# Attention with mixture of experts on one core: router constants at launch, a held load, padded router weights, seven warm-ups, a later split order and a single last eviction

## The chip, the cores and the metric

The kernel runs on one core of one Trainium2 chip. The metric is device time in microseconds of one launch, from runs of the same program; lower is better. The engines are TensorE (PE, with its weight loads as PEld), VectorE (DVE), ScalarE (ACT), GpSimd (POOL) and SyncE (SP), whose queue issues nearly all loads.

## The reference

Causal attention over 4 batches of 12 heads, 448 positions and 64 features, and then a mixture of 8 experts over the 1792 tokens that it leaves, 768 to 1024 to 768 features. A token goes to one expert only: all logits are sorted, and each in turn assigns its token to its expert if the token is still free and the expert has fewer than 224 tokens.

```python
scores = np.where(mask, -1e9, scale * q @ k.T)
attn = exp(scores - max); attn = attn / (sum + 1e-9)
x = (attn @ v) as [1792, 768]
order = np.argsort(-(x @ w_gate).flatten())
for idx in order:
    tok, e = idx // 8, idx % 8
    if assigned[tok] >= 0 or counts[e] >= 224:
        continue
    assigned[tok] = e; counts[e] += 1
for e in range(8):
    m = assigned == e
    out[m] = np.maximum(x[m] @ w1[e], 0.0) @ w2[e]
```

## The kernel before, in words

**Order of work.** One class, `Schedule`, is a list planner. Each piece of work is a task with an engine, a duration, a priority, a latency that its users see and the tasks that it waits for. `run` simulates the engines with these numbers and calls the tasks in the order that comes out, so each engine gets a fixed instruction stream, carried out in order. The durations and latencies are written by hand. A load's last number but one in `weights` (0.95 or 2.5) is the latency that the planner assumes between a weight load's slot on the DMA engines and the first use. A changed number changes the order in which instructions stand on the engines, never what they compute.

**Attention** works on 24 pairs of heads (pair 0 to pair 23). Queries and keys of a pair are one load of 512 KB into `raw` (two pairs to a tile, four tiles); pair 0's comes in three pieces (L217, L207), the first of 576 columns, 288 KB. SP's queue issues them in the order pair 0's pieces, pair 1, pair 2, V of pair 0 (`v`, L224), pair 3, V of pair 1, and then loads of two pairs each. For each pair TensorE makes scores (L236, L244), VectorE adds the mask and takes the row minimum of the negated scores (L253), ScalarE takes exponentials with their sums (L260), GpSimd shifts a block of them (L275) and collects the sums (`rs`, L269 and L270), VectorE takes reciprocals (L325), TensorE transposes the probabilities (L290), VectorE or ScalarE copies them to `PT` (L294, L296), and TensorE multiplies them by V (L318). Ahead of the first scores TensorE runs `WARM` matmuls of 512 columns on zeros (L183). The router's logits of finished pairs are matmuls against `WG` (L390), a padded array [128, 6, 32] of router weights: GpSimd clears it and two DMAs on its own queue fill it (L196 to L198).

**Router constants.** `route_constants` is a generator. Its first step is a group of GpSimd iotas, memsets and selects (L684 to L699: `w`, `kf`, `trif`, `iof`, `tvf`, `on`); its later steps are small VectorE instructions on them: `tri`, `io`, `tv` (L702 to L706), `top` (L709 to L713), `kk` (L720). `extras` gives these steps to the planner as tasks of low priority on VectorE, one after the other, and the GpSimd group comes out of the first of them:

```python
more = route_constants(self.nc, self.gc, self.k, self.cs)
n = 4 + len({d.key for ds_ in DIGITS for d in ds_})
out = [(lambda: next(more, None), False)] * n
```

**Experts.** For each expert in turn the router decides in rounds of digits which expert's threshold to set (matmuls L886 to L903, decision `cd`, `most`, `cw`, `tx`, `cut`, `gq`, `run`, L895 to L951), then its tokens are gathered (L1258), turned (L1284), split into a high and a low half (`xhl`), multiplied by the first matrix, passed through relu (L1329, `HH`, and L1341, `HL`), multiplied by the second matrix (`second`, L1353) and scattered (L1376). An expert's weights are 8 chunks of 768 KB (`wr`): 0 to 3 are the first matrix, 4 to 7 the second. Each chunk is split: ScalarE's CAST makes the high half `wh` (L1243), then three VectorE subtractions make the low half `wl` (L1249). Expert 0's first matrix is used unsplit (L1314); its chunks 4 to 7 are split like all others. While expert 0 is multiplied, the router already decides on expert 1. The results of the second matrix leave PSUM through ScalarE (L1361), but for the last expert's second half, where each 384 columns go as 192 by ScalarE and 192 by VectorE (L1359), and a scatter follows for each.

## Time and profile before

| | us |
|---|---|
| median of 3 runs | 459.64 (458.16 to 461.03) |
| the profiled execution | 460.4 |
| its span, first to last instruction | 458.7 |
| TensorE busy | 445.2 (97%) |
| VectorE busy | 357.8 (78%) |
| ScalarE busy | 285.2 (62%) |
| GpSimd busy | 78.6 (17%) |

The profiled execution is one of its own, with 1.7 us outside its span. Attention lasts to about 140 us, the first routing to about 160 us, the experts to the end. In a row of the timeline the first number is the start within the span, the second the time of the group, then engine, line, operation, tiles (written <- read), shape, and the count; brackets give how long the engine had been idle and what released it. Rows that stand together may overlap, since a group's time includes the pipeline's.

### The profile page before, as it was taken

What the parts mean: (1) busy time and instruction counts of PE and PEld (TensorE: products, weight loads), DVE (VectorE), ACT (ScalarE), POOL (GpSimd) and SP (SyncE); (2) the same over time, 40 slices, a digit from 0 to 9 for tenths busy, and PEclk for the clock granted to TensorE, in tenths of its full rate; (3) what the DMA queues carried; (4) which work ended last, traced back from release to release, by engine and by line L of the source; (5) the groups of instructions that cost most, each with busy time, mean ns of one, the idle gap of its engine ahead of it and who ended that gap; (6) DMA issues with size and microseconds to landing.
All of it is one profiled execution on the core that took longest, in us unless ns stands there. A gap on an engine that the chain in (4) does not pass through costs nothing.

```text
span 458.7 us, 11572 instructions
## 1 busy us (share of the span) xinstructions
PE 445.2 (97%) x4367; PEld 382.9 (83%) x4367; DVE 357.8 (78%) x1213; ACT 285.2 (62%) x710; POOL 78.6 (17%) x196
## 2 busy tenths in 40 slices
PE   8989999999999999999999999999999999999994
PEld 4767776767677598899998999899999999999994
DVE  4798888879888557899998999999995793874500
ACT  5989999999979023546635644744662855655310
POOL 5222131312130201003003003011026101001001
PEclk9999999999999999999999999999999999999998
DMA  7974585480004874977488578848749768661001
GB/s 246 419 300 172 189 304 218 160 312 3 2 1 141 237 271 120 345 231 246 138 275 259 156 256 237 301 158 240 275 131 317 248 219 266 234 206 51 12 16 44
DMA packets 19479, 91.20 MB, mean 199 GB/s; under 512 B 2272, under 2 KB 4832, under 8 KB 18144
## 3 DMA queue, kind: packets, MB, share of 16 engines
q1 hardware_dynamic: 16272, 79.21, 51.3%
q0 software_dynamic: 2672, 11.04, 7.6%
q8 instruction: 34, 0.56, 0.5%
q10 hardware_dynamic: 480, 0.23, 0.2%
q14 instruction: 21, 0.17, 0.1%
HBM read 79.45 MB, written 11.01 MB: 197 GB/s over the span
## 4 chain that ended last, share of the span: by engine, by line
PE 29%; issue 21%; DVE 12%; DMA 2%; POOL 2%; ACT 1%; POOLq 0%; ACTq 0%
PE po L1353 13%; PE ph L1319 6%; DVE wl L1249 5%; PE ph L1323 3%; DMA wr<-in_w 2%; DVE G L784 2%; POOL out L1376 2%; PE ph L1314 2%; PE rt L886 1%; PE po L1314 1%; PE ph L1284 1%; DVE hs L1337 1%; DVE xio L379 1%; DVE xhl L1302 1%; PE ph L1276 1%
## 5 line engine op out<-in xcount | busy, mean ns | idle before, releaser
L1249 DVE TENSOR_TENSOR wl<-wr,wh 128x512 fp32r<-128x512 f32 x180 | 115.9, 681 | 11.4 <-ACT wh L1243 11.4
L1243 ACT CAST wh<-wr 128x1536 fp32r<-128x1536 f32 x60 | 88.9, 1483 | 54.7 <-DMA wr<-in_w 36.1
L1319 PE MATMUL ph<-xhl,wh 128*128 128x448 f32 x336 | 109.5, 379 | 0.0
L260 ACT ACTIVATE P<-Sm,mx 128x320 f32<-128x320 f32 (+3 forms) x168 | 87.6, 534 | 9.0 <-DVE mx L253 7.1
L1323 PE MATMUL ph<-xhl,wl 128*128 128x224 f32 x336 | 89.0, 265 | 0.0
L1353 PE MATMUL po<-wh,HH 128*112 128x384 f32 x256 | 68.3, 343 | 0.0
L1353 PE MATMUL po<-wh,HL 128*112 128x384 f32 x256 | 67.8, 341 | 0.0
L1319 PEld LDWEIGHTS ph<-xhl,wh 128*128 128x128 f32 x336 | 63.1, 188 | 5.2 <-issue 0.7
L1353 PE MATMUL po<-wl,HH 128*112 128x384 f32 x256 | 67.2, 338 | 0.0
L1323 PEld LDWEIGHTS ph<-xhl,wl 128*128 128x128 f32 x336 | 64.2, 191 | 0.0
L318 PE MATMUL s<-PT,v 128*64 128x64 f32 (+3 forms) x672 | 46.7, 290 | 1.5 <-DVE PT L296 1.5
L236 PE MATMUL s<-raw 64*128 64x320 f32 (+2 forms) x288 | 47.1, 442 | 0.1
L318 PEld LDWEIGHTS s<-PT,v 128*64 128x64 f32 x672 | 32.3, 138 | 14.6 <-issue 8.6
L1353 PEld LDWEIGHTS po<-wl,HH 128*112 128x112 f32 x256 | 44.1, 175 | 0.3
L1353 PEld LDWEIGHTS po<-wh,HL 128*112 128x112 f32 x256 | 43.3, 175 | 0.2
L1353 PEld LDWEIGHTS po<-wh,HH 128*112 128x112 f32 x256 | 43.0, 175 | 0.3
L1258 POOL DMA_INDIRECT xio<-xd,idx x16 | 20.7, 1295 | 125.7 <-DVE acc L984 114.0
L253 DVE CUSTOM_DVE_ANT_0 Sm<-s,MK 128x320 f32<-128x320 f32 (+2 forms) x72 | 33.2, 486 | 9.3 <-PE s L236 8.9
L1337 DVE TENSOR_TENSOR hs<-ph,hc 128x224 f32<-128x224 f32 x56 | 21.6, 386 | 22.5 <-ACT hc L1333 22.2
L1376 POOL DMA_INDIRECT out<-xio,idx x15 | 15.5, 1036 | 128.1 <-ACT xio L1361 126.6
L1329 ACT ACTIVATE HH<-hs 128x224 fp32r<-128x224 f32 x56 | 21.9, 391 | 23.7 <-DVE hs L1337 23.7
L236 PEld LDWEIGHTS s<-raw 64*128 64x128 f32 x288 | 28.7, 187 | 6.7 <-DVE PT L296 2.2
(186 smaller groups left out, 669.9 us busy)
## 6 DMA issues: line engine op xcount, KB each, us to landing
wr<-in_w SPq DMA_DIRECT2D x64, 768.0 KB, 5.0
raw<-in_qk SPq DMA_DIRECT2D x10, 1024.0 KB, 10.7
v<-in_v SPq DMA_DIRECT2D x11, 896.0 KB, 9.8
xd<-xio SPq DMA_DIRECT2D x2, 1152.0 KB
xd<-xio SPq DMA_DIRECT2D x3, 576.0 KB, 3.5
raw<-in_qk SPq DMA_DIRECT2D x3, 512.0 KB, 7.8
v<-in_v SPq DMA_DIRECT2D x2, 448.0 KB, 8.8
xd<-xio SPq DMA_DIRECT2D x2, 192.0 KB, 5.2
```

The costliest lines, as they stand in the source:

```text
L236: self.nc.tensor.matmul(ts[sd][:, o:o + m], q[:, QS[i]:QS[i] + P], k, start=True, stop=True)
L253: self.nc.vector.tensor_tensor_reduce(Sm[:, QO[i] + sd * m:QO[i] + sd * m + m], self.S.pop((pp, sd, i)), mk, -0.125, 3.0e38, OP.add, OP.mi ...
L260: self.nc.scalar.activation(X[:, s], Sm[:, s], AF.Exp, bias=mx[:, o], scale=-1.0, accum_out=rw[:, o])
L318: self.nc.tensor.matmul(self.AV[pp][sd * 64:sd * 64 + 64, w:w + m], v[:, j if j < 3 else 3 + (3, 2, 0, 1)[j - 3], :], PT[:, o:o + m], star ...
L1243: self.nc.scalar.copy(hi, self.R[p, c])
L1249: self.nc.vector.tensor_sub(lo[:, s], self.R[p, c][:, s], hi[:, s].bitcast(F32))
L1319: nc.tensor.matmul(t[:, :2 * CAP], hi[:, s], x[:, d].rearrange("p z t -> p (z t)"), start=d == 0, stop=False)
L1323: nc.tensor.matmul(t[:, :CAP], lo[:, s], x[:, d, 0], start=False, stop=d == 5)
L1329: self.nc.scalar.activation(self.HH[p][:, f], self.P[p, f][:, :CAP], AF.Relu)
L1337: self.nc.vector.tensor_tensor(t, self.P[p, f][:, :CAP], self.Hc.pop((p, f)), op=OP.add)
L1353: self.nc.tensor.matmul(self.T[p, "o", u][z][:, :384], a[p][:, f, u * C:u * C + C], w[:, o:o + 384], start=f == 0 and n == 0, stop=f == 7 ...
L1376: s = self.nc.gpsimd.indirect_dma_start(out=out, in_=rows, in_offset=None, out_offset=bass.IndirectOffsetOnAxis(ap=ap, axis=0))
```

## The change

Six edits. (1) `WARM` goes from 10 to 7. (2) Pair 2's load waits until pair 0's first half load has landed; SP's queue holds everything behind it meanwhile. (3) The padded router weights are made on the host, as [128, 6, 32], and one load of 96 KB on SP's queue, behind V of pair 1, replaces the clearing and the two DMAs on GpSimd; the logits' matmuls wait for it. (4) The GpSimd group of the router constants is issued in `Attention.__init__`, ahead of the router's own memsets, and the extras are one step shorter. (5) The planner's latency of expert 0's chunks 4 to 7 is 2.5 in place of 0.95. (6) The last expert's second half leaves PSUM in one ScalarE copy per 384 columns.

```diff
--- before.py
+++ after.py
@@ -33,7 +33,7 @@
 W = 1024
 LATE = 12
 PIECES = {14: 3, 17: 3, 20: 3, 22: 2, 23: 1}
-WARM = 10
+WARM = 7
 FILL = 0.217
 SETS = ((0, 4), (4, 4), (8, 4), (12, 4), (16, 4), (20, 2), (22, 2))
 BIG = 1.0e30
@@ -193,9 +193,9 @@
         for z in range(2):
             self.nc.gpsimd.tensor_copy(self.MQ[64 * z:64 * z + 64], self.MK[64 * z:64 * z + 64, S - 128 + 64 * z:S - 64 + 64 * z])
         self.WG = self.cs.tile([128, 6, 32], F32, name="WG")
-        nc.gpsimd.memset(self.WG, 0.0)
-        nc.gpsimd.dma_start(self.WG[0:64, :, 0:E], wgP[0])
-        nc.gpsimd.dma_start(self.WG[64:128, :, E:2 * E], wgP[1])
+        self.wgP = wgP
+        self.more = route_constants(nc, gc, k, self.cs)
+        next(self.more)
 
     def bank(self):
         return self.ps.tile([P, 512], F32, name="s", bufs=8)
@@ -205,17 +205,25 @@
             self.raw = self.ld.tile([128, 2, W], F32, name="raw")
         o = p0 % 2
         if p0:
-            self.nc.sync.dma_start(self.raw[:, o:o + w], self.qk[:, p0:p0 + w])
+            a = self.nc.sync.dma_start(self.raw[:, o:o + w], self.qk[:, p0:p0 + w])
+            if p0 == 2:
+                self.tc.add_manual_dep(a.ins, self.gate.ins.name, mybir.DependencyInfo(mybir.DependencyClass.Sync, mybir.DependencyReason.DATA),
+                                       reason="first loads land first")
         else:
             self.nc.sync.dma_start(self.raw[:, 0, QS[2]:], self.qk[:, 0, QS[2]:])
         for u in range(w):
             self.QK[p0 + u] = self.raw[:, o + u]
 
+    def load_wg(self):
+        self.nc.sync.dma_start(self.WG, self.wgP)
+
     def load0(self):
         self.raw = self.ld.tile([128, 2, W], F32, name="raw")
         self.QK[0] = self.raw[:, 0]
         for a, b in ((P, QS[2]), (0, P)):
-            self.nc.sync.dma_start(self.raw[:, 0, a:b], self.qk[:, 0, a:b])
+            d = self.nc.sync.dma_start(self.raw[:, 0, a:b], self.qk[:, 0, a:b])
+            if a:
+                self.gate = d
 
     def load_v(self, g, u0=0, n=4):
         if u0 == 0:
@@ -485,6 +493,7 @@
                 prev = got[p] = add("DMA", 0.9 if p else 0.4, lambda p=p: self.load(p, 1), [prev], 9.0, 2.2)
             else:
                 prev = gotv[p] = add("DMA", 0.9, lambda p=p: self.load_v(0, 2 * p, 2), [prev], 9.0, 2.2)
+        prev = self.wg = add("DMA", 0.25, self.load_wg, [prev], 9.0, 2.2)
         for g in range(1, NP // 2):
             free = []
             if g >= 4:
@@ -627,7 +636,7 @@
         for p0, m in SETS:
             if p0 + m - 1 == pp:
                 pr = 5.9 - 0.1 * pp
-                t = self.pe(0.95, lambda: self.logits_mm(p0, m), [self.xts[p0 + u] for u in range(m)] + self.room(1), 3)
+                t = self.pe(0.95, lambda: self.logits_mm(p0, m), [self.xts[p0 + u] for u in range(m)] + [self.wg] + self.room(1), 3)
                 c = self.add("ACT/DVE", {"ACT": 0.42, "DVE": 0.56}, lambda e: self.logits_cp(e, p0, m), [t], pr + 0.3)
                 self.ring.append([c])
                 self.lts = c
@@ -659,8 +668,8 @@
                 return
 
     def extras(self, rt):
-        more = route_constants(self.nc, self.gc, self.k, self.cs)
-        n = 4 + len({d.key for ds_ in DIGITS for d in ds_})
+        more = self.more
+        n = 3 + len({d.key for ds_ in DIGITS for d in ds_})
         out = [(lambda: next(more, None), False)] * n
         self.G = self.cs.tile([P, REST, 128], BF, name="Ge")
         e = rt.early(self.G, self.wk)
@@ -1106,7 +1115,7 @@
                 deps += self.use[g - 4] if g < 8 else self.lo[g - 4]
             if p == 0 and c > 0:
                 deps.append(self.again)
-            self.got[g] = add("DMA", 2.185, lambda p=p, c=c: self.fetch(p, c), deps, 4.0 - 0.01 * g, 0.95 if p == 0 else 2.5, 1.1)
+            self.got[g] = add("DMA", 2.185, lambda p=p, c=c: self.fetch(p, c), deps, 4.0 - 0.01 * g, 0.95 if g < 4 else 2.5, 1.1)
             if g < 4:
                 self.lo[g] = [self.got[g]] * 3
                 continue
@@ -1205,12 +1214,7 @@
                            6.0 - 0.5 * p)
                 self.use.setdefault(g, []).append(prev)
             if f == 7:
-                if p == E - 1 and u == 1:
-                    a = [add(e, 0.3, lambda p=p, u=u, z=z, h=h, c=c: self.evict(p, u, z, h, c), [prev], 9.0)
-                         for z in zs for h, (e, c) in enumerate((("ACT", self.nc.scalar.copy),
-                                                                 ("DVE", self.nc.vector.tensor_copy)))]
-                else:
-                    a = [add("ACT", 0.41, lambda p=p, u=u, z=z: self.evict(p, u, z), [prev], 9.0) for z in zs]
+                a = [add("ACT", 0.41, lambda p=p, u=u, z=z: self.evict(p, u, z), [prev], 9.0) for z in zs]
                 puts.append(a)
                 if len(zs) == 1:
                     a = a + [half]
@@ -1353,11 +1357,7 @@
             self.nc.tensor.matmul(self.T[p, "o", u][z][:, :384], a[p][:, f, u * C:u * C + C], w[:, o:o + 384],
                                   start=f == 0 and n == 0, stop=f == 7 and n == 2)
 
-    def evict(self, p, u, z, h=None, copy=None):
-        if h is not None:
-            s = slice(h * 192, h * 192 + 192)
-            copy(self.IO[p][:, 2 + u, z * 384:z * 384 + 384][:, s], self.T[p, "o", u][z][:, s])
-            return
+    def evict(self, p, u, z):
         self.nc.scalar.copy(self.IO[p][:, 2 + u, z * 384:z * 384 + 384], self.T[p, "o", u][z][:, :384])
 
     def halves(self, p):
@@ -1413,10 +1413,13 @@
     v = np.pad(v, ((0, 0), (0, 0), (0, 64), (0, 0))).reshape(B, H, NC, 2, 64, D)
     own = np.stack([v, np.concatenate([v[:, :, :, :1], np.zeros_like(v[:, :, :, 1:])], axis=3)], axis=2)
     v = np.stack([own[:, 0::2], own[:, 1::2, :, :, ::-1]], axis=2).reshape(B, H, 2 * NC, 128, D)[:, :, [0, 1, 2, 4, 5, 6, 7]]
+    wg = np.zeros((2, D, 6, 4, E), np.float32)
+    for z in range(2):
+        wg[z, :, :, z] = inputs["moe_w_gate"].reshape(6, 2, D, E)[:, z].transpose(1, 0, 2)
     arrays = {
         "in_qk": np.ascontiguousarray(qk.transpose(1, 0, 2)),
         "in_v": np.ascontiguousarray(v.transpose(3, 0, 1, 2, 4)),
-        "in_wg": np.ascontiguousarray(inputs["moe_w_gate"].reshape(6, 2, D, E).transpose(1, 2, 0, 3)),
+        "in_wg": np.ascontiguousarray(wg.reshape(128, 6, 32)),
         "in_w1": np.ascontiguousarray(inputs["moe_w1"].reshape(E, 6, 128, 4, 256).transpose(0, 2, 3, 1, 4)).reshape(
             E, 128, 4, 1536),
         "in_w2": np.ascontiguousarray(inputs["moe_w2"].reshape(E, 4, 2, 128, DM).transpose(0, 3, 1, 2, 4)).reshape(
```

TensorE's and ScalarE's order in the attention is the same but for the three warm-ups. On VectorE the constants' steps stand one place earlier. The first piece is VectorE between pair 2's last row minimum `mx` and the copies `PT` (`rs` is pair 2's sums; `tri`, `io`, `tv`, `top` are the constants). Before:

```order
L253 ISA mx 128x1
L325 RECIPROCAL rs<-rs 128x8
L702 CAST tri<-trif 128x128
L704 TENSOR_SCALAR io<-iof 128x224
L706 CAST tv<-tvf 128x14
L296 COPY PT<-s 128x6x64
L296 COPY PT<-s 128x7x64
```

After, in the same place:

```order
L261 ISA mx 128x1
L711 CAST tri<-trif 128x128
L713 TENSOR_SCALAR io<-iof 128x224
L715 CAST tv<-tvf 128x14
L333 RECIPROCAL rs<-rs 128x8
L718 TENSOR_SCALAR top<-kf 128x128
L720 TENSOR_SCALAR kkx<-top 128x128
L721 TENSOR_TENSOR top<-top,kkx 128x128
L722 MEMSET top 128x1
L304 COPY PT<-s 128x6x64
L304 COPY PT<-s 128x7x64
```

The three casts of constants moved ahead of the reciprocal, and `top`'s four instructions ahead of the two copies.

The second piece is VectorE at expert 1's decision, beside expert 0's matrices (`wl` is the low half of expert 0's chunk 4, `HL` the low half of its relu). Before:

```order
L895 TENSOR_SCALAR cd_119<-rt 64x8
L1249 TENSOR_TENSOR wl<-wr,wh 128x512
L909 TENSOR_REDUCE most<-rt 128x1
L911 SCALAR_TENSOR_TENSOR cw<-rt,most,w_418 128x8
L913 TENSOR_REDUCE tx<-cw 128x1
L915 TENSOR_SCALAR cut<-kw,most 128x14
L921 TENSOR_SCALAR ei<-tx 128x1
L917 TENSOR_SCALAR cut<-kw,most 128x14
L940 SCALAR_TENSOR_TENSOR gq<-tm,tx,cut 128x28
L944 SCALAR_TENSOR_TENSOR run<-on,gq 128x28
L1341 SCALAR_TENSOR_TENSOR HL<-ph,HH 128x224
L951 TENSOR_REDUCE pos<-rt 128x14
```

After:

```order
L904 TENSOR_SCALAR cd_133<-rt 64x8
L918 TENSOR_REDUCE most<-rt 128x1
L920 SCALAR_TENSOR_TENSOR cw<-rt,most,w_108 128x8
L922 TENSOR_REDUCE tx<-cw 128x1
L924 TENSOR_SCALAR cut<-kw,most 128x14
L930 TENSOR_SCALAR ei<-tx 128x1
L926 TENSOR_SCALAR cut<-kw,most 128x14
L949 SCALAR_TENSOR_TENSOR gq<-tm,tx,cut 128x28
L953 SCALAR_TENSOR_TENSOR run<-on,gq 128x28
L1345 SCALAR_TENSOR_TENSOR HL<-ph,HH 128x224
L1253 TENSOR_TENSOR wl<-wr,wh 128x512
L960 TENSOR_REDUCE pos<-rt 128x14
```

The split of chunk 4 moved from ahead of the whole decision to behind `run` and one `HL`. On ScalarE the CAST of chunk 5 stands behind three relus of expert 0 in place of two, and that of chunk 7 behind the casts of `xhl`. From expert 1 on, the order is shuffled in many places, with the same number of instructions.

## Rows read from the trace of the kernel before

**Rows 1.** Busy time by stretch: us, PE, PEld, DVE, ACT, POOL, granted clock, DMA share, GB/s.
```profile
5.00:10.00 5.00, 4.89 (x34) 2.42 (x32) 3.36 (x19) 2.83 (x11) 2.49 (x6) 1.00 1.01 344
10.00:20.00 10.00, 9.58 (x134) 6.81 (x132) 8.96 (x43) 10.00 (x36) 1.58 (x7) 1.00 1.01 408
60.00:80.00 20.00, 20.00 (x326) 14.76 (x321) 16.64 (x65) 19.28 (x65) 5.13 (x19) 1.00 0.67 247
250.00:300.00 50.00, 49.46 (x422) 45.36 (x421) 49.04 (x159) 29.25 (x47) 4.48 (x6) 1.00 0.74 232
```

**Rows 2.** Waits of TensorE: who waited for whom, us in total, times, longest.
```profile
PE s L318 <- DVE PT L296: 1.5, 1, 1.5
...
PE rt L947 <- DVE gq L940: 1.0, 1, 1.0
```

**Rows 3.** Timeline of the launch, 1 to 11 us.
```profile
1.30 4.45 PE L183 MATMUL s<-zero 128*128 128x512 bf16 x10 [1.30 <-DVE zero L180]
...
5.04 0.69 POOL L198 DMA_DIRECT2D WG<-in_wg  x1
5.68 1.89 PE L236 MATMUL s<-raw 64*128 64x320 f32 x12
...
7.17 0.56 ACT L260 ACTIVATE P<-Sm,mx 128x320 f32<-128x320 f32 x1 [4.86 <-DVE mx L253]
...
7.93 1.17 PEld L236 LDWEIGHTS s<-raw 64*128 64x128 f32 x12 [0.24 <-DMA raw<-in_qk]
7.94 1.89 PE L236 MATMUL s<-raw 64*128 64x320 f32 x12
...
10.95 0.29 POOL L275 COPY P<-P 64x128 f32<-64x128 f32 x1 [3.46 <-ACT P L260]
```

**Rows 4.** DMA issues, loads of raw: queue, count, KB each, median us to landing.
```profile
raw<-in_qk SPq DMA_DIRECT2D x3, 512.0 KB, 7.8
...
raw<-in_qk SPq DMA_DIRECT2D x1, 288.0 KB, 3.0
```

**Rows 5.** Timeline of pair 2 to pair 4, 21 to 31 us.
```profile
21.50 0.15 POOL L684 IOTA w<- 128x8 f32 x1
...
22.69 1.52 POOL L693 IOTA iof<- 128x256 f32 x1
22.76 1.53 DVE L702 CAST tri<-trif 128x128 f16<-128x128 f32 x1 [1.10 <-POOL trif L690]
...
24.73 0.20 POOL L699 MEMSET on<- 128x128 f16 x1
24.80 0.18 DVE L706 CAST tv<-tvf 128x14 f16<-128x14 f32 x1 [0.29 <-POOL tvf L697]
24.89 1.08 DVE L296 COPY PT<-s 128x384 f32<-128x384 f32 x2
...
26.03 1.12 PE L318 MATMUL s<-PT,v 128*64 128x256 f32 x20 [1.48 <-DVE PT L296]
...
26.47 0.56 ACT L260 ACTIVATE P<-Sm,mx 128x320 f32<-128x320 f32 x1 [1.05 <-POOL rs L270]
...
30.08 0.29 DVE L712 TENSOR_TENSOR top<-top,kkx 128x128 int32<-128x128 int32 x1
```

**Rows 6.** Timeline of expert 1's decision, 173 to 177 us.
```profile
173.48 1.47 ACT L1243 CAST wh<-wr 128x1536 fp32r<-128x1536 f32 x1 [2.48 <-DMA wr<-in_w]
...
173.71 0.17 PE L898 MATMUL rt<-cd,on 128*128 128x8 f16 x1
...
174.99 0.69 DVE L1249 TENSOR_TENSOR wl<-wr,wh 128x512 fp32r<-128x512 f32 x1 [1.41 <-ACT wh L1243]
...
176.88 0.17 PE L947 MATMUL rt<-gq,tri 128*128 128x28 f16 x1 [1.01 <-DVE gq L940]
```

**Rows 7.** Timeline of the tail, 444 to 455 us.
```profile
444.03 0.86 ACT L1361 COPY xio<-po 112x384 f32<-112x384 f32 x2 [7.01 <-PE po L1353]
...
452.56 0.36 DVE L1359 COPY xio<-po 112x192 f32<-112x192 f32 x1 [3.81 <-PE po L1353]
452.95 0.32 ACT L1359 COPY xio<-po 112x192 f32<-112x192 f32 x1 [3.85 <-DVE xio L1359]
...
453.55 0.94 POOL L1376 DMA_INDIRECT out<-xio,idh  x1 [3.14 <-ACT xio L1359]
```

## The prediction

> **What bounds the kernel now.** I read the busy time by stretch first. Between 60 and 80 us TensorE is busy 20.00 of 20.00 us, and between 250 and 300 us 49.46 of 50.00, with VectorE at 49.04 beside it [rows 1]. A busy TensorE is a pipelined figure of the profile, so it doesn't say that every matmul runs at its best; it does say that TensorE waits for almost nothing there. So what counts is where TensorE stands when such a stretch begins: time won ahead of it is carried to the end. The opening is different: ScalarE is busy 10.00 of 10.00 us between 10 and 20 us, TensorE 9.58 [rows 1], so there the exponentials set the pace. Next I read TensorE's list of waits: two of its long ones, 1.5 us for the copies PT and 1.0 us for the router's `gq` [rows 2], lie at places that the diff touches. Then I read the timeline at four places: the launch [rows 3], with the loads by size [rows 4] beside it, pair 2 to pair 4 [rows 5], expert 1's routing decision [rows 6], and the tail [rows 7].
>
> **The change part by part.** The sum is made against the profiled run, 460.4 us (span 458.7 and 1.7 around it), which stands 0.76 us above the median of 459.64.
>
> *Launch.* The ten warm-ups run from 1.30 us until the first scores start at 5.68 us [rows 3]: 4.38 / 10 = 0.438 us each. Three fewer let the scores start at 5.68 - 1.31 = 4.37 us. Their data is there: the first half load takes 3.0 us from its issue [rows 4], which falls in the first microsecond, so it lands before 4 us. How much of the 1.31 us lasts depends on two things. First, the clock. A warm-up of 512 columns in 0.438 us is 1.2 columns per ns, the lower of the two levels (1.2 and 2.4 GHz). The first and the second set of 12 scores both take 1.89 us [rows 3] and the granted clock is 1.00 between 5 and 10 us [rows 1]: the upper level is reached by the first scores, at about 5.7 us, after 4.4 us of warm-up. If it rises at the same moment when scores stand there in place of warm-ups, the scores between 4.37 and 5.7 us go at half rate, and 1.31 / 2 = 0.65 us is won; if it is up at 4.37 us, all of 1.31. Second, pair 1's load: its scores start at 7.93 us after a wait of 0.24 us for that load [rows 3], so scores that end earlier meet a load that must also land earlier. That is what the hold on pair 2 is for: the three loads of 512 KB take 7.8 us to land [rows 4], while the DMA share is 1.01 between 5 and 10 us [rows 1]: they share full engines. Held behind the first half load, pair 2's bytes come about 3 us later and pair 1 has the engines to itself. Ahead of pair 2 then lie 1024 KB (pair 0's pieces of 288, 64 and 160 KB and pair 1's 512 KB), at 344 GB/s [rows 1] 3.0 us of transfer. I estimate that pair 1 lands between 6.3 us (bytes flowing from 3.3 us on) and 7.0 us (the last of it shared with pair 2) instead of 7.9. The Trainium skill ("DMA: Bandwidth & Descriptors", section "Two DMAs through the same engine are not ordered") says that descriptors of one queue on one DMA engine start in order. By that pair 2 never took anything from pair 1, and the hold could do nothing. The loads of 7.8 us beside one of 3.0 us [rows 4] do not decide it, since each also waits for those ahead. Behind the held load SP's whole queue waits: V's first load, pair 3, V's second, the router weights, all up to 3 us late in their issue. As the engines are full from 5 us on, the landing moves only by the time in which they run dry, between 0 and about 0.5 us, an estimate; ScalarE's backlog covers that. ScalarE's first exponential stands at 7.17 us [rows 3], and as it sets the pace until 20 us, it passes on what the scores win. Bounds: 0 (pair 1 lands no sooner and nothing else moves) to 1.31; I take -0.7, the half-rate figure.
>
> *Router weights.* A memset and two DMA issues (the second 0.69 us) leave GpSimd [rows 3], and one load of 96 KB joins SP's queue: 0.28 us at 344 GB/s, ahead of V loads that are needed much later. Cost 0, hidden by ScalarE's pace; 0.28 if not.
>
> *GpSimd's constants.* Before, they run from 21.50 to 24.93 us, 3.43 us [rows 5], and VectorE waits in its order for them: 1.10 us for `trif`, then a CAST of 1.53 us beside GpSimd's IOTA of 1.52 us (the small CAST of `tv` takes 0.18, `io` 0.28), then 0.29 us for `tvf` [rows 5]. Behind them stand the copies PT, at 24.89 us, and behind these TensorE, idle 1.48 us, and ScalarE, idle 1.05 us [rows 5]. With the constants ready since launch VectorE saves 1.10 + 0.29 + (1.53 - 0.29) = 2.63 us. Against that, the planner now puts the four instructions of `top` ahead of these copies: at most 4 x 0.29 = 1.16 us [rows 5]. The copies come 1.47 us or more earlier, against TensorE's idle 1.48 us: -1.4, bounds -1.0 (ScalarE's own idle time) and -1.5. At launch GpSimd must hold 3.43 us more, less the two issues (2 x 0.69 = 1.38 or more) gone: 2.05 us. Between 5 and 10 us it is idle 5.00 - 2.49 = 2.51 us [rows 1], and it is first waited for at 10.95 us, by pair 0's shift [rows 3]. Cost 0; if the cover were gone, up to 0.7.
>
> *Expert 0's second matrix.* Before, VectorE's split of chunk 4 stands ahead of expert 1's decision. It waits 1.41 us for ScalarE's CAST, which itself had waited for its load, and `most` and its followers stand behind it, up to `gq`, for which TensorE waits 1.01 us at 176.88 us, although its matmul of the digits' counts was done at 173.88 us [rows 6]. In the new order `most` stands directly behind `cd` and could start at about 174.1 us, some 1.5 us earlier: the wait of 1.01 us goes. The split is made after `run` and HL; it is wanted only when the second matrix begins, behind the rest of the first one on TensorE, so nothing is late next. Taken: -1.0. From both sides: the order of experts 1 to 7 is shuffled too, with the same counts. A new wait of the size of the old one would give +0.5 (1.5 lost, 1.0 won); half of TensorE's idle 0.54 us per 50 us [rows 1] over the 250 us of those experts would be a further -1.3, so -2.3.
>
> *Tail.* Before, VectorE's half (0.36 us), then ScalarE's half (0.32 us), then the scatter: from 452.56 to 453.55, 0.99 us [rows 7]. One copy of 384 takes 0.86 / 2 = 0.43 us, and the scatter starts 453.55 - 452.95 - 0.32 = 0.28 us after [rows 7]: 0.71. -0.28, bounds -0.1 and -0.4. Nothing follows but the scatter.
>
> Sum: 0.7 + 1.4 + 1.0 + 0.28 = 3.38; 460.4 - 3.38 = 457.02 for a run like the profiled one, and 0.76 lower at the median: **456.3 us**.
>
> **The rivals.** One per cent of 459.64, about what a measurement of this kernel can tell from no change, is 4.6 us: 455.0 and 464.2.
> - *The hold gives nothing.* Pair 1 lands at 7.9 us whatever stands behind it; only ScalarE's backlog moves forward, and the launch is worth about 0.2: 456.8. For it: all these loads go out on one queue, in the order of issue; against it: full engines and 7.8 us for a load.
> - *The new order stalls elsewhere.* VectorE is full (49.04 of 50), so each split put later can hold a decision of a later expert, as this one did. Price 1.5, all that the edit won and half again: 457.8. For it: the planner's latency is a number set by hand; against it: TensorE waited only 0.54 us in 50 [rows 1].
> - *More is won.* 1.3 + 1.5 + 2.3 + 0.3 = 5.4: 454.2.
> - *The clock rises late, milder and slower case.* Seven warm-ups end at 4.37 us, and scores wait and pause more than warm-ups do. If the upper level comes at x instead of 5.7 us, TensorE's work up to x takes twice as long and (x - 5.7) / 2 is lost. A rise after pair 1's scores, at about 9.8 us, costs 2.1: 458.4. The whole gain of 3.4 is gone at x = 12.5 us, and from x = 21.5 us, where 7.9 is lost, the kernel is slower by over 1%: 464.3. For it: rows 3 show the rise only after ten. The Trainium skill ("TensorE: Matmul & The Clock Gate", section "What's actually happening") has "the default state is throttled, and activity releases the throttle"; by that fewer warm-ups may delay the rise. Against it: from 4.37 us on scores of the same engine follow with a gap of 0.24 us at most, which are activity as well.
>
> **How the numbers follow.** Forecast 0.50 (own range 454.5 to 457.8), hold worth nothing 0.10, new stalls 0.17, more won 0.13, late clock 0.07 at 458.4 and 0.03 beyond 464.2. Below 455.0 lie three tenths of the forecast's own case (0.15), most of the case that wins more (0.11) and a little of the others (0.06): 0.32. Slower by over 1%: the late clock's 0.03 and 0.01 for new stalls at several experts. The range leaves out the best of "more" below and the clock's worst above: 453.4 to 459.6.
>
> **What would show it.** Right: first scores at about 4.4 us with sets of 12 that take over 1.89 us until about 5.7; pair 1's scores at 6.9 to 7.3 us; the wait PT L296 gone from TensorE's list; the CAST of `tri` at some 0.3 us; `most` about 0.2 us behind L898's matmul; 0.71 us between the last product and the last scatter. Wrong: pair 1's scores at 7.9 us; a second and third set of scores that take 3.8 us, or a granted clock under 1.00 between 5 and 20 us; GpSimd's shift later than the last exponential of its pair; new waits of over 1 us between 200 and 440 us.

## The result, and the profile after

The changed kernel takes 455.12 us at the median of 6 runs (454.86 to 455.92), the kernel before 459.23 us beside it (458.16 to 461.03, 6 runs). The ratio is 0.9912, with a 95% interval from 0.989 to 0.9934: 4.1 us or 0.9% faster, 0.8 us more than was forecast. Two more sets of runs of the same kernel gave 0.9913 and 0.9912. The profiled execution has a span of 453.2 us and took 454.86 us; against the profiled 460.4 us of before that is 5.5 us, of which some 1.4 us is not the change, since the profiled run of before lies above its median and that of after a little below.

Busy time by stretch, of the changed kernel, with the columns of [rows 1]:

```profile
5.00:10.00 5.00, 5.00 (x44) 3.13 (x40) 3.85 (x19) 3.48 (x13) 3.52 (x9) 1.00 0.98 360
10.00:20.00 10.00, 9.65 (x142) 6.87 (x140) 9.25 (x45) 10.00 (x36) 1.74 (x8) 1.00 1.03 418
60.00:80.00 20.00, 20.00 (x297) 14.07 (x296) 17.52 (x73) 19.27 (x68) 5.90 (x22) 1.00 0.54 200
250.00:300.00 50.00, 49.73 (x427) 45.70 (x427) 47.92 (x162) 28.75 (x46) 6.23 (x9) 1.00 0.61 196
```

What bounds each stretch is as before: ScalarE is busy 10.00 of 10.00 us between 10 and 20 us, TensorE 20.00 of 20.00 us in the attention and 49.73 of 50.00 in the experts. GpSimd has 3.52 us of work between 5 and 10 us in place of 2.49, so the constants fit into time in which it was idle.

TensorE's list of waits, where both rows of [rows 2] are gone:

```profile
PE s L183 <- DVE zero L180: 1.3, 1, 1.3
PE po L353 <- ACT n L824: 0.7, 1, 0.7
PE ph L1288 <- DMA xio<-xd,idx: 0.4, 1, 0.4
PE rt L912 <- DVE cd L909: 0.4, 2, 0.2
PE s L298 <- ACT P L268: 0.2, 1, 0.2
```

The timeline of the launch, against [rows 3]:

```profile
1.29 3.17 PE L183 MATMUL s<-zero 128*128 128x512 bf16 x7 [1.29 <-DVE zero L180]
...
4.39 2.89 PE L244 MATMUL s<-raw 64*128 64x320 f32 x12
...
6.52 0.56 ACT L268 ACTIVATE P<-Sm,mx 128x320 f32<-128x320 f32 x1 [4.21 <-DVE mx L261]
...
7.48 1.89 PE L244 MATMUL s<-raw 64*128 64x320 f32 x12
```

The first scores stand at 4.39 us, 1.29 us earlier. The first 12 take 2.89 us and the next 12 1.89 us, so part of the first set ran at the lower of TensorE's two levels. The first exponential stands 0.65 us earlier (7.17 to 6.52) and pair 1's scores 0.46 us (7.94 to 7.48). TensorE is 0.66 us earlier from 11 us on.

The timeline of pair 2 and 3, against [rows 5]:

```profile
19.92 0.30 DVE L711 CAST tri<-trif 128x128 f16<-128x128 f32 x1
...
20.32 0.16 DVE L715 CAST tv<-tvf 128x14 f16<-128x14 f32 x1
...
21.46 0.29 DVE L721 TENSOR_TENSOR top<-top,kkx 128x128 int32<-128x128 int32 x1
...
21.79 0.55 DVE L304 COPY PT<-s 128x384 f32<-128x384 f32 x1
...
22.85 1.93 PE L326 MATMUL s<-PT,v 128*64 128x384 f32 x28
```

The waits for GpSimd are gone, the CAST of `tri` takes 0.30 us in place of 1.53, and the copies PT start at 21.79 us in place of 24.89. The second group of TensorE's matmuls with V, which had waited, runs on behind the first in one row (x28). TensorE stands 2.36 us earlier behind it than before, 0.66 of which came from the launch; at 60 us, and from there to the end of the attention, it stands 2.55 us earlier, so that 1.89 us come from here.

The timeline of expert 1's decision, against [rows 6]:

```profile
170.30 1.47 ACT L1247 CAST wh<-wr 128x1536 fp32r<-128x1536 f32 x1 [2.13 <-DMA wr<-in_w]
...
170.87 0.17 PE L907 MATMUL rt<-cd,on 128*128 128x8 f16 x1
...
171.11 0.17 DVE L918 TENSOR_REDUCE most<-rt 128x1 f32<-128x8 f32 x1 [0.36 <-PE rt L907]
...
172.81 0.68 DVE L1253 TENSOR_TENSOR wl<-wr,wh 128x512 fp32r<-128x512 f32 x1
172.87 0.18 PE L956 MATMUL rt<-gq,tri 128*128 128x28 f16 x1
```

`most` follows its matmul at once (171.04 to 171.11 us), no longer behind a split that waits for the CAST, and TensorE's matmul on `gq` has no wait.

The timeline of the tail, against [rows 7]:

```profile
447.42 0.48 ACT L1361 COPY xio<-po 112x384 f32<-112x384 f32 x1 [3.69 <-PE po L1357]
448.18 0.94 POOL L1376 DMA_INDIRECT out<-xio,idh  x1 [3.14 <-ACT xio L1361]
```

From the start of the copy to the scatter 0.76 us, in place of 0.99.

### The profile page after: what moved, and what is told of

It is laid out like the page before. It is cut to its first block, busy times and chain, and to the rows that moved or that the text cites. A ratio compares the mean times of both kernels' runs of the same rounds, so it can differ in the third digit from the quotient of the medians.

```text
span 453.2 us, 11557 instructions
## 1 busy us (share of the span) xinstructions
PE 443.9 (98%) x4364; PEld 382.8 (84%) x4364; DVE 357.0 (79%) x1211; ACT 285.6 (63%) x710; POOL 76.2 (17%) x193
## 4 chain that ended last, share of the span: by engine, by line
PE 29%; issue 21%; DVE 13%; DMA 2%; POOL 2%; ACT 2%; POOLq 0%; SPq 0%; ACTq 0%
PE po L1357 11%; PE ph L1323 6%; DVE wl L1253 5%; PE ph L1318 3%; PE ph L1327 3%; DVE G L793 2%; POOL out L1376 2%; PE rt L895 1%; DMA wr<-in_w 1%; PE po L1318 1%; PE ph L1288 1%; PE ph L1280 1%; DMA xio<-xd,idx 1%; DVE xio L387 1%; DVE xhl L1306 1%
## 5 line engine op out<-in xcount | busy, mean ns | idle before, releaser
L1247 ACT CAST wh<-wr 128x1536 fp32r<-128x1536 f32 x60 | 88.6, 1482 | 56.1 <-DMA wr<-in_w 45.9
L261 DVE CUSTOM_DVE_ANT_0 Sm<-s,MK 128x320 f32<-128x320 f32 (+2 forms) x72 | 33.3, 486 | 8.8 <-PE s L244 8.3
```

Of the source, the lines that this page charges most:

```text
L261: self.nc.vector.tensor_tensor_reduce(Sm[:, QO[i] + sd * m:QO[i] + sd * m + m], self.S.pop((pp, sd, i)), mk, -0.125, 3.0e38, OP.add, OP.mi ...
L1247: self.nc.scalar.copy(hi, self.R[p, c])
```

## The experiments

Twelve kernels ran, in four groups; the kernels of a group ran on one chip, beside the kernel before. The medians of the kernel before in the four groups were 459.8, 458.89, 460.07 and 459.86 us, so a difference is taken within a group. Where TensorE is said to stand earlier or later in one profile than in another, the starts of the same instruction are compared.

### Four parts by themselves

**Ten warm-ups in the changed kernel** (`a_warm10`).

```diff
-WARM = 7
+WARM = 10
```

> The changed kernel with ten warm-ups again, all else as changed. Theory (ScalarE's exponentials set the pace of the opening, so what counts is when the first scores end): first scores at 5.7 us, first exponential at 7.17 us as in the kernel before, 0.65 us later than in the changed kernel, and everything on TensorE behind it up to the end 0.65 us later; median 0.4 to 0.8 us above the changed kernel's. Rival (the held load does it: pair 1 lands sooner and that is what moves TensorE): pair 1's scores at 7.7 us or sooner, and TensorE from 12 us on within 0.2 us of the changed kernel. Rival (clock): ten warm-ups give all scores the upper level, pair 0's scores end at 7.7 us as before and nothing is lost against seven: difference under 0.2 us.

Measured: 457.35 us (456.85 to 458.01), ratio 0.9949 (0.993 to 0.9967). **The changed kernel without the hold** (`a_nohold`):

```diff
-            if p0 == 2:
-                self.tc.add_manual_dep(a.ins, self.gate.ins.name, ...)
```

> The changed kernel without the wait on pair 2's load. Theory (pair 0's exponentials occupy ScalarE until about 10.1 us, and pair 1's first mask would be ready some 0.4 us before that even with pair 1 landing as late as in the kernel before): pair 1's load lands at 7.7 to 7.9 us in place of 7.2, its scores start at about 7.9 us, but ScalarE's exponentials and TensorE from 12 us on stay within 0.1 us of the changed kernel; median within 0.3 us. Rival (the prediction: the hold is needed to keep the launch's gain): TensorE 0.4 to 0.5 us later from 12 us to the end. Rival (descriptors of one queue start in order, so pair 2 takes nothing from pair 1): pair 1 lands at 7.2 us also without the wait.

Measured: 456.91 us (456.21 to 458.59), ratio 0.9934 (0.9916 to 0.9952). Both ratios are higher than the changed kernel's 0.9912, but neither time can be set against 455.12, which comes from another chip; both were run again beside the changed kernel (below). The profile with ten warm-ups is not what was expected: the first scores stand at 5.00 us and the first exponential at 6.49, not at 5.7 and 7.17, and up to 140 us TensorE stands within 0.03 us of the changed kernel's first profile. So this profile alone shows no price of the three warm-ups. The profile without the hold speaks against the rival that pair 2 takes nothing: TensorE waits 2.0 us for pair 1's load, whose scores start at 8.95 us, and stays 0.67 us later than in the changed kernel's first profile to the end of the attention.

**The constants alone** (`b_const`, from the kernel before):

```diff
         nc.gpsimd.dma_start(self.WG[64:128, :, E:2 * E], wgP[1])
+        self.more = route_constants(nc, gc, k, self.cs)
+        next(self.more)
...
-        more = route_constants(self.nc, self.gc, self.k, self.cs)
-        n = 4 + len({d.key for ds_ in DIGITS for d in ds_})
+        more = self.more
+        n = 3 + len({d.key for ds_ in DIGITS for d in ds_})
```

> The kernel before with the router constants alone moved: GpSimd's group issued at launch, behind the two DMAs of the router weights, and the extras one step shorter. Theory: nothing changes up to 25 us; the wait of 1.48 us at L318 goes and TensorE stands 1.7 us earlier at 27 us and 1.9 us earlier (2.3 at 31 us, part given back by 42 us) up to 140 us; median 457.3, which is 1.9 below the kernel before. Rival (the wait is replaced by ScalarE's own pace): 1.0 us earlier at 140 us. Rival (GpSimd's longer launch is not covered, since here its two DMA issues stay): pair 0's shift later than 10.95 us and 0.3 to 0.7 us given back.

Measured: 458.2 us (456.37 to 459.88, 12 runs), 1.6 below the kernel before, ratio 0.9966 (0.9948 to 0.9984). In its profile the launch happened to be 0.64 us later than in that of before, and at 140 us TensorE was 1.22 us earlier: 1.86 us won by the constants, as the theory has it. The IOTA of `iof` takes its 1.52 us here with no CAST beside it, and GpSimd is ready before pair 0's shift though its two DMA issues stayed:

```profile
6.95 1.52 POOL L695 IOTA iof<- 128x256 f32 x1
...
10.60 0.16 POOL L738 MEMSET cd<- 128x18 f16 x2
11.58 0.29 POOL L277 COPY P<-P 64x128 f32<-64x128 f32 x1 [0.82 <-ACT P L262]
```

The CAST of `tri` takes 0.29 us here. It took 1.53 us in each of the three profiles in which it runs beside that IOTA (the kernel before, `b_lat`, `b_wgtail`) and 0.28 to 0.30 us in the others, so the long CAST goes with the IOTA, though no run takes the IOTA alone away. The cover on GpSimd holds: its shift waits for ScalarE.

**The order alone** (`b_lat`, from the kernel before):

```diff
-... 0.95 if p == 0 else 2.5, 1.1)
+... 0.95 if g < 4 else 2.5, 1.1)
```

> The kernel before with the planner's latency of expert 0's chunks 4 to 7 alone changed to 2.5. Theory: TensorE as before up to 160 us; the wait of 1.0 us for gq at 177 us goes, and of the 2.3 us that the changed kernel wins behind 160 us nearly all appears here: 1.1 us at the decision and the rest in experts 0 to 2; median 2.3 us below the kernel before (2.0 to 2.6). Rival (only the wait on the decision counts): 1.0 us. Rival (what the changed kernel wins behind 200 us comes from loads that come earlier because attention ends earlier, not from the order): 1.1 us at 180 us and no more at 440 us.

Measured: 459.23 us (457.9 to 460.42, 12 runs), 0.57 below, ratio 0.9987 (0.9973 to 1.0), so it is not clear of no change. In its profile the wait for gq is gone and TensorE is 2.5 us earlier at 200 us than its own launch would have it, but 1.6 us of that are lost between 300 and 330 us. My 2.3 us was wrong: it had been read off two single profiles.

### The changed kernel again, the old order in it, and four warm-ups

**The changed kernel unaltered** (`after_again`).

> The changed kernel itself, unaltered, beside the next kernels on one chip. The undoing runs show waits behind 240 us (ScalarE's hc 2.1 us late at 244 us, TensorE's wait for cd at 317 us) that the changed kernel's profile doesn't have, although every engine's order is the same. Theory (these waits come and go with the moments at which loads and semaphores land, not with what was undone): here the attention stands 0.7 +- 0.7 us earlier by the launch and 1.9 by the constants, and some of those waits appear in the profile; ratio to the kernel before between 0.990 and 0.994. Rival (the changed kernel is free of them by its shorter launch): no wait over 0.5 us on TensorE behind 200 us, ratio 0.991 again.

Measured: 455.18 us (454.17 to 456.41), ratio 0.9913 (0.9891 to 0.9936). One such wait appears, 0.7 us at 294 us for `hs`, and the ratio stands. So the waits behind 240 us come and go in the same program, as the theory has it.

**The changed kernel with the old latency** (`a_oldlat`): the line of `b_lat` undone.

> The changed kernel with the planner's old latency of 0.95 for expert 0's chunks, so with the old order in the experts. Theory from the run of the latency alone, which won only 0.6 us at the median: 0.4 to 0.8 us above the changed kernel, with a wait on gq at 173 us of 0.3 to 1.0 us and with the old order's waits at 192 us (counts behind xhl) and 248 us, each 0.6 us. Rival (the order is worth what the changed kernel's profile shows behind 160 us): 2.3 us above. Rival (with the attention 2.5 us earlier the old order no longer stalls at the decision): within 0.2 us of the changed kernel.

Measured: 455.75 us (454.64 to 456.38), ratio 0.9922 (0.9901 to 0.9942): 0.57 us above the changed kernel of its group, the same 0.57 as from the other side, and again not clear of noise (the two intervals overlap). The waits that were expected at 192 and 248 us did not come. The wait for gq is back, in the same shape as in [rows 6]:

```profile
170.72 1.47 ACT L1247 CAST wh<-wr 128x1536 fp32r<-128x1536 f32 x1 [2.38 <-DMA wr<-in_w]
...
172.23 0.69 DVE L1253 TENSOR_TENSOR wl<-wr,wh 128x512 fp32r<-128x512 f32 x1 [1.31 <-ACT wh L1247]
...
174.13 0.17 PE L956 MATMUL rt<-gq,tri 128*128 128x28 f16 x1 [0.92 <-DVE gq L949]
```

**Four warm-ups** (`a_warm4`): `WARM = 4` in the changed kernel.

> The changed kernel with four warm-ups in place of seven. The first scores can't start before the first half load, 3.9 us, against 4.39 us with seven. Theory (the moment of the clock's rise doesn't follow the warm-ups' count one by one; it varies between 4.2 and 7.1 us in the runs so far, and ScalarE's first exponential follows the first scores): first scores at 4.0 to 4.1 us at the lower level, first exponential at 6.1 to 6.5 us, TensorE from 12 us on 0 to 0.4 us earlier than in the changed kernel; median within 0.5 us. Rival (the late clock: fewer warm-ups delay the rise to behind pair 0's scores): scores of pair 0 and pair 1 at half rate, first exponential later than 6.6 us, 0.5 to 2 us above the changed kernel.

Measured: 455.68 us (454.95 to 456.36), ratio 0.9927 (0.9907 to 0.9946), 0.5 above the changed kernel of its group, within noise. The timeline of its launch:

```profile
1.29 1.89 PE L183 MATMUL s<-zero 128*128 128x512 bf16 x4 [1.29 <-DVE zero L180]
...
3.85 3.57 PE L244 MATMUL s<-raw 64*128 64x320 f32 x12 [0.67 <-DMA raw<-in_qk]
...
5.97 0.56 ACT L268 ACTIVATE P<-Sm,mx 128x320 f32<-128x320 f32 x1 [3.67 <-DVE mx L261]
...
7.76 1.99 PE L244 MATMUL s<-raw 64*128 64x320 f32 x8
```

The first 12 scores take 3.57 us, nearly twice 1.89, and pair 1's first 8 alone 1.99 us: pair 0's scores and the first of pair 1's ran at the lower level. The first exponential, at 5.97 us, is earlier than in most profiles with seven, yet TensorE stands 0.8 to 1.1 us later than in the changed kernel's first profile at pair 0's transposes and 0.35 us later from 20 us on (0.67 us later than in `after_again`, of the same chip). So TensorE is later, not 0 to 0.4 us earlier as the theory had it. This one profile shows the late clock of the rival, though not its late first exponential.

### Warm-ups and hold beside the changed kernel, and the two small edits

The changed kernel (`after_c`), with ten warm-ups (`a_warm10_c`) and without the hold (`a_nohold_c`), with the edits shown above:

> The changed kernel once more, so that the next two can be set against it on the same chip (the first runs that undo the warm-ups or the hold ran on another chip than the changed kernel did). Theory (the changed kernel's gain is the same on every chip): ratio 0.990 to 0.993. Rival (the waits behind 240 us that the undoing runs showed belong to the chip): ratio 0.994 to 0.996 if this chip has them, with ScalarE's hc 2 us late near 243 us in the profile.

> The changed kernel with ten warm-ups, beside the changed kernel on the same chip. Theory (first scores at 4.4 us in place of 5.0 to 5.7 us, of which the clock's low level takes back about half): 0.3 to 0.9 us above the changed kernel at the median. Rival (the moment of the clock's rise decides, and is no later with seven than with ten): 0 +- 0.3 us. Rival (what the first such run showed, ratio 0.9949 against 0.9912, was the warm-ups): 1.7 us above.

> The changed kernel without the wait on pair 2's load, beside the changed kernel on the same chip. Theory (pair 2's packets share the engines with pair 1's; without the wait pair 1 lands 0.7 to 1.4 us later and TensorE from 12 us on stands 0.4 to 0.8 us later to the end of attention): 0.4 to 0.9 us above the changed kernel at the median. Rival (ScalarE's backlog covers it): within 0.2 us.

Measured: 455.72 us (455.3 to 456.02), 456.5 (455.65 to 458.13) and 456.37 (455.79 to 456.6), ratios 0.9912 (0.9894 to 0.9931), 0.9933 (0.9911 to 0.9955) and 0.9928 (0.9912 to 0.9944). So the warm-ups are worth 0.78 us and the hold 0.65 us at the median. By the scatter of the runs the means differ by 1.0 +- 0.8 us for the warm-ups and 0.7 +- 0.4 us for the hold, and the ratios of the first pair of runs would give 1.7 and 1.0 us; the sizes are rough, but the profiles bear out both. First scores, first exponential and pair 1's scores of the changed kernel:

```profile
4.39 1.93 PE L244 MATMUL s<-raw 64*128 64x320 f32 x12
...
5.94 0.56 ACT L268 ACTIVATE P<-Sm,mx 128x320 f32<-128x320 f32 x1 [3.63 <-DVE mx L261]
...
7.25 1.89 PE L244 MATMUL s<-raw 64*128 64x320 f32 x12 [0.66 <-DMA raw<-in_qk]
```

The same with ten warm-ups:

```profile
1.29 4.32 PE L183 MATMUL s<-zero 128*128 128x512 bf16 x10 [1.29 <-DVE zero L180]
...
5.54 1.89 PE L244 MATMUL s<-raw 64*128 64x320 f32 x12
...
7.04 0.56 ACT L268 ACTIVATE P<-Sm,mx 128x320 f32<-128x320 f32 x1 [4.73 <-DVE mx L261]
```

And without the hold:

```profile
5.89 0.56 ACT L265 ACTIVATE P<-Sm,mx 128x320 f32<-128x320 f32 x1 [3.59 <-DVE mx L258]
...
8.52 1.51 PE L241 MATMUL s<-raw 64*128 64x320 f32 x10 [1.98 <-DMA raw<-in_qk]
```

With ten warm-ups the first exponential is 1.10 us later, and TensorE 1.06 us later at 120 us. Without the hold the first exponential is as early as with it, but pair 1's scores wait 1.98 us for their load and start 1.27 us later; ScalarE's backlog covers some 0.5 of that, and TensorE is 0.79 us later at 120 us.

**Router weights and tail alone** (`b_wgtail`, from the kernel before): edits (3) and (6) of the change.

> The kernel before with two edits that stand far apart in time: the padded router weights by one load on SP's queue, and the single ScalarE copy for the last 384 columns. Theory: no shift on TensorE from 12 us to the end of the second matrix beyond the launch's own variation (the clock's rise between 4.2 and 7.1 us); from the last product to the last scatter 0.71 to 0.77 us in place of 0.99; median 0.2 to 0.3 us below the kernel before, not clear of noise. Rival (96 KB more on SP's queue delay V of pairs 2 and 3): a wait of TensorE or PT on a load between 12 and 35 us and 0.3 us lost.

Measured: 459.19 us (458.37 to 461.1, 12 runs), ratio 0.9985 (0.997 to 0.9999). That is 0.88 us below the kernel before at the median, three times what was expected, with an interval from 0 to 1.4 us by the ratio. The tail is as expected:

```profile
451.56 0.48 ACT L1358 COPY xio<-po 112x384 f32<-112x384 f32 x1 [3.69 <-PE po L1350]
452.31 0.94 POOL L1373 DMA_INDIRECT out<-xio,idh  x1 [3.13 <-ACT xio L1358]
```

0.75 us in place of 0.99, which accounts for 0.24 of the 0.88. No wait for `v` or the router weights appears between 12 and 140 us. This kernel has the old order, but no wait for gq: chunk 4's load landed earlier here, ScalarE's CAST was done at 173.58 us, and the split began before the decision's matmul did, so that `most` starts 0.25 us behind that matmul (174.23 us) and not 1.71 us as in the kernel before:

```profile
172.11 1.47 ACT L1240 CAST wh<-wr 128x1536 fp32r<-128x1536 f32 x1 [1.00 <-DMA wr<-in_w]
173.62 0.69 DVE L1246 TENSOR_TENSOR wl<-wr,wh 128x512 fp32r<-128x512 f32 x1
...
173.81 0.17 PE L900 MATMUL rt<-cd,on 128*128 128x8 f16 x1
...
174.23 0.16 DVE L911 TENSOR_REDUCE most<-rt 128x1 f32<-128x8 f32 x1
```

### A version that might have been better

**Pair 1's load in two pieces** (`a_split1`), since TensorE still waits for it where the clock is early:

```diff
+        if p0 == 1:
+            for s in (slice(0, QS[2]), slice(QS[2], W)):
+                self.nc.sync.dma_start(self.raw[:, 1, s], self.qk[:, 1, s])
-        if p0:
+        elif p0:
```

> The changed kernel with pair 1's load in two pieces (704 columns, 352 KB, and then 320 columns, 160 KB), as a version that might beat it. In four of the changed kernel's and its relatives' launches TensorE waits 0.4 to 0.7 us for pair 1's load. Theory (pair 1's landing bounds the launch where the clock rises early): the first piece lands 0.3 to 0.5 us sooner, at 6.7 to 6.9 us, that wait shrinks to 0.3 us or less, and TensorE from 12 us on is 0 to 0.4 us earlier; ratio to the kernel before 0.990 to 0.9915. Rival (ScalarE's backlog covers what is left of the wait): no shift from 12 us on, 0.991 to 0.992. Rival (one more issue on SP's queue pushes pair 2 and V back): a wait for raw or v behind 10 us, ratio over 0.992.

Measured: 455.76 us (454.97 to 456.69), ratio 0.9916 (0.9895 to 0.9937): the changed kernel's own ratio. In its profile the first 12 scores took 3.15 us, so the clock rose late, there was no wait for the load to take away, and what the split would do in an early launch stays open. No run beats the changed kernel.

## Why the prediction was right, and by how much its terms were off

The forecast of 456.3 us, 0.6 to 0.7% under the kernel before, met 455.12 us and a ratio of 0.9912. The parts add up within their noise: 0.78 (warm-ups) + 0.65 (hold) + 1.6 (constants) + 0.57 (order) + 0.23 (tail) = 3.8 us, against 4.1, 3.7 and 4.35 us in the three sets of runs of the whole. The first four are medians, each uncertain by 0.4 to 0.9 us; the tail is read from the profile, since `b_wgtail` gave 0.88 us at the median. That the forecast is met within 0.8 us is in part luck: the launch was put 0.7 us too low and the order 0.4 us too high, and these two partly cancel.

*Launch*, taken as 0.7: it is some 1.4, the term that was mis-sized most. Three steps failed. "If it rises at the same moment": there is no such moment. Six profiles with ten warm-ups have their first exponential between 6.49 and 7.81 us, mean 7.28; seven with seven between 5.89 and 6.52, mean 6.26. The mean difference is 1.0 us, not 0.65; in four of the seven the first set, which starts at 4.39 us, takes 1.89 to 2.26 us, so the upper level came early in it. Next, the hold was counted as what lets the launch keep its gain, with pair 1 at 7.9 us without it. Without it pair 1's scores stood at 8.52 and 8.95 us in two profiles of the changed kernel and at 8.43 to 8.70 us in the three profiles of the kernel before with one or two edits; the 7.94 us of [rows 3] is the earliest of six, so the hold has a gain of its own. And the hold is short: the prediction has pair 2's bytes about 3 us later, but V's first load, the next in SP's queue, is issued only 1.1 us later. Before:

```profile
3.16 0.43 SPq L224 DMA_DIRECT2D v<-in_v  x1
```

After:

```profile
4.29 0.43 SPq L232 DMA_DIRECT2D v<-in_v  x1
```

The 3 us are what the first half load takes from its own issue at 0.82 us to its landing at 3.77 us; pair 2's load is issued at 2.69 us in the kernel before, so the hold can only move it by the 1.1 us between. The estimate of pair 1's landing, 6.3 to 7.0 us, was a little early: where its scores waited for it they start at 7.23 to 7.53 us.

*The hold gives nothing*, the rival with 0.10, fell: with the same queue and the same order, pair 1's scores start 1.27 us later when pair 2 is issued without waiting. The rule of the Trainium skill ("DMA: Bandwidth & Descriptors", section "Two DMAs through the same engine are not ordered") speaks of the start of descriptors within one engine's queue. That pair 2 can take nothing from pair 1 does not follow from it, and here the load in front landed later all the same.

*Router weights*, taken as 0: nothing in the traces speaks against it, but no run separates it from the tail, and the 0.88 us of the two together leave room for a gain that is not shown.

*Constants*, taken as 1.4 with an upper bound of 1.5: 1.6 at the median, and 1.86 and 1.89 in the attention of two profiles. The CAST's share, 1.53 - 0.29, was right (0.30 us alone). The step that failed is the upper bound, TensorE's wait of 1.48 us: the end of the matmuls ahead of it is modelled, and once the wait was gone TensorE stood 1.70 us earlier than the launch alone had put it. The charge of 1.16 us for `top` was too high as well, since the copies PT start 2.44 us earlier behind the launch, not 1.47.

*Expert 0's order*, taken as 1.0: 0.57, from both sides, neither clear of noise. The wait itself was read rightly, and `a_oldlat` shows it again with 0.92 us. Two steps failed. One is that the 1.01 us stand in every run: of four profiles with the old order two have the wait (the kernel before, `a_oldlat`) and two don't (`b_const`, `b_wgtail`), where chunk 4's load landed earlier against the decision. The other is that "nothing is late next". TensorE makes the same matmuls in both orders, so its time between points with the same work behind them can be compared in all profiles; the points are named by their place in the changed kernel's first profile.

| stretch, us | old order, 4 profiles | new order, 10 profiles |
|---|---|---|
| 165 to 198 | 34.0 to 35.2 | 33.0 to 33.3 |
| 198 to 280 | 82.0 to 82.8 | 81.8 to 82.9 |
| 280 to 336 | 55.5 to 55.6 | 56.1 to 58.2 |

In the first stretch, which holds the decision, the new order wins 0.7 us or more even where the old one has no wait for gq; between 280 and 336 us it gives back 0.6 to 2.7 us, in every profile. The 0.57 is what is left of the two.

*New stalls*, the rival with 0.17, is thus true beside the forecast: its loss is there, but smaller than the gain. Only a part of it shows as waits. With the new order TensorE waits for `cd`: 0.4 us in all in the first profile, and in that of `after_c`, with 0.7 us at 316 us,

```profile
PE rt L912 <- DVE cd L909: 1.2, 3, 0.7
```

The old order has such waits too, here in `b_wgtail`:

```profile
PE rt L905 <- DVE cd L902: 0.7, 2, 0.5
...
PE rt L888 <- DVE G L786: 0.5, 1, 0.5
```

What holds the new order up in the rest of that stretch stays open.

*Tail*, taken as 0.28: 0.23, since the copy of 384 took 0.48 us where 0.43 was put down.

*The late clock*, the slower rival: with seven warm-ups the first set of scores took at most 3.15 us and the second 1.89 us, so the rise never came behind pair 0's scores. In the one profile with four it did. That kernel's 0.5 us at the median is not clear of noise; in the profile TensorE's delay shrinks from 0.8 us at 12 us to 0.35 us at 20 us, the stretch in which ScalarE sets the pace, so less is left than (x - 5.7) / 2 would have it.

## What to carry to other kernels

A wait seen in one profile is worth its length only if it stands in every run and nothing behind it gives the time back. The wait for GpSimd's constants brought its whole length (1.6 us for 1.48). The wait that hangs on a load's landing stood in two of four profiles, and the new order loses part of its gain 100 us later (0.57 us for 1.01). In an opening where transfers fill the DMA engines, it can pay to hold back the load that is needed later: issue order on one queue did not protect the load in front here, and about 1 us of delay brought it in 1.27 us sooner. Small constant work belongs where its engine is idle, and its price elsewhere includes what it slows beside it (a CAST of 0.30 us took 1.53 us beside an IOTA).

## What was not expected of the hardware

The moment at which TensorE reaches the upper level varies in the same program. Ten warm-ups from 1.30 us took 4.45 us before, 4.32 us in `a_warm10_c` and 3.77 us in `a_warm10`, so in the last it rose while they ran; seven were followed by 12 scores in 1.89 to 3.15 us. The windows of the profile tell a granted clock of 1.00 for 1.30 to 4.20 us all the same: at the launch the durations have to be read, not that column. The Trainium skill ("TensorE: Matmul & The Clock Gate", section "What's actually happening") says that the same kernel can show different numbers of slow matmuls from run to run; the traces agree, and here it is a first exponential that moves by 1.3 us among six launches with ten warm-ups.

In the seven profiles of the new order that come from two of the chips, one copy `hc` of ScalarE starts late. In `a_warm10`, `a_nohold` and `b_lat`, all of one chip, it starts about 1.7 us after the matmul that it needs, with no work on this core that released it:

```profile
244.25 0.34 ACT L1337 COPY hc<-ph 128x224 f32<-128x224 f32 x1 [2.09 <-remote]
```

In `after_c`, `a_warm10_c`, `a_nohold_c` and `a_split1`, of another chip, the same copy starts about 0.9 us after its matmul (ScalarE idle for 1.30 to 1.32 us), and in `after`, `after_again` and `a_warm4` at once (0.42 to 0.43 us). The instructions stand in the same order in all ten. VectorE, TensorE and the decision behind it wait in turn (0.6 us at L895 in `a_warm10`), and of the ten the same seven, and only they, have TensorE idle for 0.7 to 0.8 us ahead of its matmul on `cd` at 316 to 320 us. The cause of both stays open.
